# Attention with agents and a two-layer product on one core: the main loop in the order it is written, with jobs at fixed places

## The chip, the cores and the metric

The kernel runs on one core of a Trainium2 chip. A core has a matrix engine (TensorE, PE in the profile; its weight loads are PEld), VectorE (DVE), ScalarE (ACT), GpSimd (POOL) and a queue that issues transfers (SyncE, SP). Each engine takes its own instructions strictly in order; between engines they wait on semaphores. TensorE writes to PSUM, which VectorE and ScalarE read. The metric is the time of one execution on the device in microseconds, lower is better.

## The reference

Four batches of 12480 tokens with 128 channels, 49 agents, and a hidden width of 2048:

```python
def sm(a, b):                       # softmax over the last axis
    s = scale * (a @ b.transpose(0, 2, 1))
    e = np.exp(s - s.max(-1, keepdims=True))
    return e / (e.sum(-1, keepdims=True) + 1e-09)
agent_v = sm(agents, k) @ v         # phase 1: each batch, over all keys
x = (sm(q, agents) @ agent_v).reshape(49920, 128)
h = x @ w_in                        # phase 2: all tokens
out = (h - np.tanh(h)) @ w_out
```

## The kernel before

`sm(q, agents) @ agent_v @ w_in` is computed as `sm(q, agents) @ (agent_v @ w_in)`, so that the first product of phase 2 has only 49 rows to sum over; `aw` is that small matrix of one batch. Products that need more than the fast f32 format gives are made from a rounded part and a rest: `awh` and `awl`, `wo_h` and `wo_l`, `gh` and `gl`, stacked or added as several matmuls.

The tokens are cut into 100 blocks of 500 (25 a batch), and a block's hidden width into 8 pairs of 128 columns. One **step** is one block and one column pair, 800 steps in all; two blocks make a pair of blocks, 16 steps, and `pos` counts 0 to 15 in it. A step has on TensorE the first product (`m1`, L536/L537, 4 matmuls into the PSUM tile `h`, three buffers), on ScalarE tanh and its square (`act`, L546 `y` and L548 `z`), on VectorE the multiplication `g = h * z` (L551), on GpSimd the rounding `gh` of `g` (`high`, L580), on VectorE the rest `gl = g - gh` (`low`, L586), and on TensorE the second product (`m2`, L599 to L601, 6 matmuls into `misc`). The tanh difference is approximated by `h` times a scaled square. All steps of the first block and one step in every even block are **f32 steps**: no rounding and no rest, 2 f32 matmuls (recorded as 4, L597) with `g` itself. That step is column pair 7 (`PLAIN_PAIR`).

Beside the steps run **jobs**, Python generators that are advanced by one `yield` a step:

- the queries of the next pair of blocks (`q_softmax`): 64 small matmuls (L492), maximum (L500), copy (L501), subtraction on GpSimd (L503), exponential (L505), sum, reciprocal and multiplication on VectorE (L507 to L510, the normalization), rounding (L513) and rest on GpSimd (L515); then a transpose per block (L523, L528);
- phase 1 of the next batch, three jobs started in each pair of blocks: 13 score jobs (64 small matmuls L278, a copy and a maximum), the maximum over all, 13 value jobs (subtraction on GpSimd L321, exponential L329, 16 matmuls L341, an addition on VectorE L354), then `aw` of that batch in four projections (L456 to L460).

PSUM tiles of jobs and the accumulator of the second product share two buffers (`misc`).

The order on each engine comes from a scheduler that simulates the program, within limits that the kernel gives it: `hold` puts an instruction behind another on the same engine, `burst` and `streamed` tie small matmul groups of jobs to the stream of large ones on TensorE, `issue_order` fixes the early part. The products of the steps themselves are free to pass one another.

Of the kernel before, what the change touches and what calls it, by code (L numbers as in the profile page):

```python
# [57 lines left out]
PLAIN_PAIR = NCH // 2 - 1  # L58
PLAIN_EVERY = 2
LAG1 = 1  # L60
LAG2 = 2
# [3 lines left out]
SPLIT = (8, 9, 11, 13)  # L65
QL = 0
QS = 5
T0 = 13
T1 = 3
KS = (6, 9, 14)  # L70
VS = (2, 5, 9)
# [26 lines left out]
class Build:  # L98
    def __init__(self, ctx, tc, aps):
# [8 lines left out]
        self.stream = None  # L108
# [86 lines left out]
    def phase1(self, b):  # L195
# [36 lines left out]
        def scores(g):  # L232
# [41 lines left out]
            first = self.count()  # L274
# [4 lines left out]
            self.burst(first)  # L279
# [9 lines left out]
        def max_in():  # L289
# [4 lines left out]
            nc.vector.tensor_reduce(m, part, axis=AX.X, op=ALU.max)  # L294
            ps = self.misc()
# [17 lines left out]
        def av(g):  # L313
# [8 lines left out]
            if b:  # L322
                self.hold(first, self.gh_at, (ET.Pool,))
# [4 lines left out]
            first = self.count()  # L328
            nc.scalar.activation(e3, e3, AF.Exp, scale=SCALE)  # L329
            if b:  # L330
                self.hold(first, self.act_at, (ET.Activation,))
                yield
            yield
            if b:
                ps = self.misc()
                first = self.count()
# [11 lines left out]
                self.burst(first)  # L348
# [90 lines left out]
    def project(self, b, bound):  # L439
        nc = self.nc  # L440

        def part(c, lo, hi):
# [16 lines left out]
            nc.scalar.copy(h, ps)  # L459
            nc.vector.tensor_tensor(awl[:A2, sl], ps, h.bitcast(F32), ALU.subtract)  # L460
# [20 lines left out]
    def q_softmax(self, halves, qt, res, TT=TT):  # L481
        nc = self.nc
        yield
        ps = self.misc()
        first = self.count()
# [7 lines left out]
        self.burst(first)  # L493
        yield
# [7 lines left out]
        yield  # L502
        nc.gpsimd.tensor_tensor(ev, ev, m[:TT, :, None].broadcast_to([TT, GT, A]), ALU.subtract)  # L503
        yield
        nc.scalar.activation(ev, ev, AF.Exp, scale=SCALE)  # L505
        yield
# [4 lines left out]
        yield  # L511
        pp = self.small.tile([128, GT, A2], F32R, tag="pp", name="pp")
        nc.scalar.copy(pp[:TT, :, :A], ev)  # L513
        yield
        nc.gpsimd.tensor_tensor(pp[:TT, :, A:], ev, pp[:TT, :, :A].bitcast(F32), ALU.subtract)  # L515
        res.append(pp)
# [26 lines left out]
    def act(self, h, w):  # L543
# [5 lines left out]
        self.act_at = self.last_name()  # L549
        g = self.wtile("g", NB["g"])[:, : 2 * w]  # L550
        nc.vector.tensor_tensor(self.pair(g), h, self.pair(z), ALU.mult)  # L551
# [26 lines left out]
    def high(self, g):  # L578
        gh = self.wtile("gh", NB["gh"])[:, : g.shape[1]].bitcast(F32R)
        self.nc.gpsimd.tensor_scalar(gh, g, 1.0, 0.0, ALU.mult, ALU.add)  # L580
        self.gh_at = self.last_name()
        return gh
# [38 lines left out]
    def queued(self, first):  # L621
        return [i for i in list(self.nc.cur_bb.bb.instructions)[first:] if i.engine == ET.PE]

    def after(self, i, names):
        info = mybir.DependencyInfo(mybir.DependencyClass.NoSync, mybir.DependencyReason.DATA)
        for name in names:
            self.tc.add_manual_dep(i, name, info, reason="order on TensorE")
# [309 lines left out]
```

## Time and profile before

| | us |
|---|---|
| median of 3 runs | 2156.54 (2156.36 to 2161.76) |
| profiled execution, its own time | 2154.2 |
| its span in the profile | 2152.4 |
| busy in the span: TensorE, weight loads | 2089.7 (97%), 1635.8 (76%) |
| VectorE, ScalarE, GpSimd | 1989.5 (92%), 1795.2 (83%), 1378.3 (64%) |

Until 57.7 us phase 1 of the first batch runs. The first multiplication `g` starts there. Then the 50 pairs of blocks follow, the last one at 2106.9 us. From 1723.4 us on there is no more phase 1 to do, only steps and query jobs. Reading the profile: a row of the groups gives line, engine, operation, tiles and shapes, then count, busy us, mean ns of one, and idle time of the engine before them with what ended it. A row of the waits is who waited, for whom, us in total, times, and longest. A matmul's record covers its way through the array, so that consecutive records overlap.

### The profile page before, as it was taken

Reading aid. Unit: us, or ns where it says so; the run is one execution under the profiler, and the core shown is the slowest. Engines: PE = TensorE matmul, PEld = TensorE weight load, DVE = VectorE, ACT = ScalarE, POOL = GpSimd, SP = SyncE. Lnnn points to the kernel's source line nnn. Section 1 sums busy time; section 2 is a strip of 40 time slices with the busy share of each in tenths; the row PEclk is TensorE's granted clock in tenths of the full one; section 3 lists DMA queues with packets and bytes.
Section 4 is the critical chain, followed back from the end, with each engine's and each line's share of the span. In section 5 each row is a group of like instructions: output and inputs, shape, how many; then the busy total and the mean of one; then the engine's idle time right before and its main releaser. Section 6 shows DMA issues by size and latency. Waiting matters only on the chain.

```text
span 2152.4 us, 38228 instructions
## 1 busy us (share of the span) xinstructions
PE 2089.7 (97%) x14885; PEld 1635.8 (76%) x14885; DVE 1989.5 (92%) x2028; ACT 1795.2 (83%) x2097; POOL 1378.3 (64%) x896
## 2 busy tenths in 40 slices
PE   8999999999999999999999999999999999999998
PEld 7577777777777777777777777877777788888886
DVE  7999998889998999889999999998989999999998
ACT  3888887788788888888888888888878989989897
POOL 0365576666665566666666656767766777777776
PEclk9999999999999999999999999999999999999999
DMA  9221102111111111112001110121000000010000
GB/s 355 91 67 62 52 29 60 59 50 40 36 53 59 52 58 40 59 44 65 31 20 59 59 52 20 49 69 41 20 29 30 20 31 28 20 39 20 30 11 21
DMA packets 65358, 109.21 MB, mean 51 GB/s; under 512 B 3984, under 2 KB 44176, under 8 KB 65168
## 3 DMA queue, kind: packets, MB, share of 16 engines
q1 hardware_dynamic: 65168, 106.68, 15.1%
q8 instruction: 119, 1.95, 0.4%
q14 instruction: 71, 0.58, 0.1%
HBM read 81.10 MB, written 25.56 MB: 50 GB/s over the span
## 4 chain that ended last, share of the span: by engine, by line
PE 70%; DVE 15%; POOL 6%; issue 6%; ACT 3%; DMA 0%; POOLq 0%; DVEq 0%; SPq 0%; ACTq 0%
PE h L536 13%; PE h L537 12%; PE misc L599 12%; PE misc L601 12%; PE misc L600 11%; DVE g L551 8%; POOL gh L580 5%; DVE gl L586 4%; PE misc L597 3%; PE misc L341 2%; ACT z L548 1%; PE misc L492 1%; ACT y L546 1%; PE misc L523 1%; PE h L249 1%
## 5 line engine op out<-in xcount | busy, mean ns | idle before, releaser
L580 POOL TENSOR_SCALAR gh<-g 128x1000 fp32r<-128x1000 f32 (+1 forms) x743 | 1218.6, 1640 | 611.2 <-DVE g L551 499.9
L586 DVE TENSOR_TENSOR gl<-g,gh 128x1000 fp32r<-128x1000 f32 (+1 forms) x743 | 937.2, 1262 | 100.4 <-POOL gh L580 91.4
L551 DVE TENSOR_TENSOR g<-h,z 128x1000 f32<-128x1000 f32 (+1 forms) x800 | 945.4, 1190 | 27.9 <-ACT z L548 24.0
L546 ACT ACTIVATE y<-h 128x1000 f32<-128x1000 f32 (+1 forms) x800 | 798.7, 1000 | 118.6 <-PE h L537 113.8
L548 ACT ACTIVATE z<-y 128x1000 f32<-128x1000 f32 (+1 forms) x800 | 831.3, 1041 | 53.4 <-DVE g L551 35.4
L536 PE MATMUL h<-pT,awh 98*128 98x500 f32 (+1 forms) x1600 | 654.5, 409 | 7.9 <-DVE g L551 7.8
L537 PE MATMUL h<-pT,awl 98*128 98x500 f32 (+1 forms) x1600 | 621.2, 388 | 0.0
L599 PE MATMUL misc<-gh,wo_l 128*128 128x500 f32 (+1 forms) x1486 | 594.6, 400 | 5.9 <-ACT o L783 3.0
L601 PE MATMUL misc<-gl,wo_h 128*128 128x500 f32 (+1 forms) x1486 | 584.9, 394 | 7.7 <-DVE gl L586 7.6
L600 PE MATMUL misc<-gh,wo_h 128*128 128x500 f32 (+1 forms) x1486 | 579.1, 390 | 0.0
L536 PEld LDWEIGHTS h<-pT,awh 98*128 98x128 f32 x1600 | 300.7, 188 | 96.3 <-DVE g L551 24.8
L537 PEld LDWEIGHTS h<-pT,awl 98*128 98x128 f32 x1600 | 302.6, 189 | 69.9 <-issue 12.4
L599 PEld LDWEIGHTS misc<-gh,wo_l 128*128 128x128 f32 x1486 | 280.5, 189 | 83.6 <-POOL gh L580 21.3
L601 PEld LDWEIGHTS misc<-gl,wo_h 128*128 128x128 f32 x1486 | 279.7, 188 | 78.4 <-DVE gl L586 23.4
L600 PEld LDWEIGHTS misc<-gh,wo_h 128*128 128x128 f32 x1486 | 280.2, 189 | 49.3 <-issue 1.1
L503 POOL TENSOR_TENSOR qe<-qe,qm 126x392 f32<-126x392 f32 x50 | 65.5, 1309 | 61.4 <-ACT qe L501 61.4
L515 POOL TENSOR_TENSOR pp<-qe,pp 126x392 fp32r<-126x392 f32 x50 | 51.6, 1031 | 67.3 <-ACT pp L513 67.3
L597 PE MATMUL misc<-g,wo_f 128*128 128x500 f32 (+1 forms) x196 | 91.4, 588 | 0.0
L783 ACT ACTIVATE o<-misc 128x500 f32<-128x500 f32 (+1 forms) x100 | 57.9, 579 | 36.4 <-PE misc L597 21.6
L501 ACT COPY qe<-misc 126x392 f32<-126x392 f32 x50 | 24.1, 482 | 74.2 <-DVE qm L500 74.2
L528 ACT CAST pT<-misc 98x500 fp32r<-98x500 f32 (+1 forms) x100 | 57.1, 572 | 11.3 <-PE misc L523 9.7
L492 PEld LDWEIGHTS misc<-ag,qt 128*32 128x32 f32 (+1 forms) x3200 | 39.3, 112 | 24.9 <-issue 17.6
(103 smaller groups left out, 829.0 us busy)
## 6 DMA issues: line engine op xcount, KB each, us to landing
kt<-kT SPq DMA_DIRECT2D x48, 512.0 KB, 3.9
qt<-qT SPq DMA_DIRECT2D x46, 500.0 KB, 3.5
outT<-o SPq DMA_DIRECT2D x46, 500.0 KB, 2.6
v<-v SPq DMA_DIRECT2D x36, 512.0 KB, 4.0
vt<-v SPq DMA_DIRECT2D x12, 512.0 KB, 7.5
raw<-w_in SPq DMA_DIRECT2D x4, 512.0 KB, 9.2
v<-w_out SPq DMA_DIRECT2D x4, 512.0 KB, 7.8
qt<-qT SPq DMA_DIRECT2D x4, 490.0 KB, 3.7
```

What stands on the lines that cost most here:

```text
L503: nc.gpsimd.tensor_tensor(ev, ev, m[:TT, :, None].broadcast_to([TT, GT, A]), ALU.subtract)
L536: nc.tensor.matmul(h[:, c, :w], aw[0][:A2, sl], pT[:A2, :w], start=True, stop=False)
L537: nc.tensor.matmul(h[:, c, :w], aw[1][:A2, sl], pT[:A2, :w], start=False, stop=True)
L546: nc.scalar.activation(self.pair(y), h, AF.Tanh, scale=TSC)
L548: nc.scalar.activation(z, y, AF.Square)
L551: nc.vector.tensor_tensor(self.pair(g), h, self.pair(z), ALU.mult)
L580: self.nc.gpsimd.tensor_scalar(gh, g, 1.0, 0.0, ALU.mult, ALU.add)
L586: self.nc.vector.tensor_tensor(gl, g, gh.bitcast(F32), ALU.subtract)
L597: nc.tensor.matmul(acc[:, :w], wf[:, c * C : (c + 1) * C], gh[:, x], start=first, stop=last)
L599: nc.tensor.matmul(acc[:, :w], self.wo_l[:, f, :], gh[:, x], start=first, stop=False)
L600: nc.tensor.matmul(acc[:, :w], self.wo_h[:, f, :], gh[:, x], start=False, stop=False)
L601: nc.tensor.matmul(acc[:, :w], self.wo_h[:, f, :], gl[:, x], start=False, stop=last)
```

## The change

The order of the loop is written out, and the engines keep it: at the end `issue_order` now fixes VectorE, GpSimd and TensorE for the whole program (before: early parts only), and `burst`, `streamed` and their bookkeeping are gone. The loop body is rewritten to fit. Step k has, in this order: jobs are advanced; tanh and square of step k+1 (`squares`); multiplication of step k (`product`); its rounding; rest of step k-1 (`low(1)`); second product of step k-1 (`out`); first product of step k+3 (`first_product`, `AHEAD = 3`); new jobs are started. Before, it was: first product of step k, jobs, tanh, square, multiplication and rounding of step k, rest of step k-1, second product of step k-3.

So jobs stand on VectorE between a subtraction (of two steps back) and a multiplication. Further:

- the f32 step is column pair 6 instead of 7, and the queries' normalization stands at `pos` 6 to 7 (`QS`, `QGAPS`);
- 87 of the 743 roundings are done by ScalarE (`by_act`): at the step after which a value job starts, and at `pos` 8 (`QLOW`), where the rest of the queries stands on GpSimd;
- GpSimd's two-tile subtractions of value jobs (L321) and of the queries' rest wait on a semaphore for the multiplication (`wait_for`), where a value job's subtraction was before only held behind the last rounding in GpSimd's own order;
- jobs start at other positions: `KS`, `VS`, `T0`, `T1`; the queries' load, still issued at `pos` 0, is used three steps later instead of six; an output block is copied two steps after its last product.

```diff
-PLAIN_PAIR = NCH // 2 - 1
+PLAIN_PAIR = 6
-QS = 5
-T0 = 13
-T1 = 3
-KS = (6, 9, 14)
-VS = (2, 5, 9)
+QS = 2
+QGAPS = (1, 1, 0, 2, 1, 1, 1)
+QLOW = 8
+T0 = 11
+T1 = 13
+KS = (3, 5, 13)
+VS = (1, 3, 11)
...
             (nc.gpsimd if b else nc.vector).tensor_tensor(e3, sv, top, ALU.subtract)
             if b:
-                self.hold(first, self.gh_at, (ET.Pool,))
+                self.wait_for(first, self.mul_at)
...
+        first = self.count()
         nc.gpsimd.tensor_tensor(pp[:TT, :, A:], ev, pp[:TT, :, :A].bitcast(F32), ALU.subtract)
+        if gaps != (1,) * 7:
+            self.wait_for(first, self.mul_at)
...
-    def high(self, g):
+    def high(self, g, act=False):
         gh = self.wtile("gh", NB["gh"])[:, : g.shape[1]].bitcast(F32R)
-        self.nc.gpsimd.tensor_scalar(gh, g, 1.0, 0.0, ALU.mult, ALU.add)
-        self.gh_at = self.last_name()
+        if act:
+            self.nc.scalar.copy(gh, g)
+        else:
+            self.nc.gpsimd.tensor_scalar(gh, g, 1.0, 0.0, ALU.mult, ALU.add)
...
+    def wait_for(self, first, name):
+        info = mybir.DependencyInfo(mybir.DependencyClass.Sync, mybir.DependencyReason.DATA)
+        for i in list(self.nc.cur_bb.bb.instructions)[first:]:
+            self.tc.add_manual_dep(i, name, info, reason="order at the shared port")
...
-            h = foreground(n, i)
+            if p + 1 < npair and pos in (T0, T1):
+                live.append(t_job(2 * p + 2 + (pos == T1)))
             nxt = []
...
-            rest(n, i, h)
-            low(LAG1)
+            self.hold(first, self.act_at, (ET.Activation,))
+            squares(k + 1)
+            values = nv - NG - 2 < len(kq) < nv
+            begin = kq and n and pos in (VS if values else KS)
+            by_act = values and begin and kq[0] is not None or p and pos == QLOW and p + 1 < npair
+            product(k, by_act)
+            low(1)
...
-            out(LAG2)
+            out(k)
             if n == 0 and i == HP - 1:
-                self.issue_order(ET.DVE, at)
                 self.issue_order(ET.Activation, at)
-                self.issue_order(ET.PE, early)
-            if p + 1 < npair:
+            first_product(k + AHEAD)
+            if p and p + 1 < npair:
...
+        self.issue_order(ET.DVE, at)
+        self.issue_order(ET.Pool, early)
+        self.issue_order(ET.PE, early)
         self.loads_first(early)
```

Three places show what moved. The first is VectorE in the second block of a pair with value jobs (steps 130 to 134; `gl` and `qm` as above, `acc` is the value job's addition). Before:

```order
L586 TENSOR_TENSOR gl_4393<-g_4364,gh_4366 128x1000
L551 TENSOR_TENSOR g_4418<-h_4407,z_4416 128x1000
L586 TENSOR_TENSOR gl_4422<-g_4389,gh_4391 128x1000
L586 TENSOR_TENSOR gl_4444<-g_4418,gh_4420 128x1000
L551 TENSOR_TENSOR g_4440<-h_4430,z_4438 128x1000
L500 TENSOR_REDUCE qm_4522<-misc_4459 126x8
L551 TENSOR_TENSOR g_4496<-h_4454,z_4494 128x1000
```

and in the change:

```order
L589 TENSOR_TENSOR gl_4460<-g_4402,gh_4404 128x1000
L494 TENSOR_REDUCE qm_4476<-misc_4419 126x8
L551 TENSOR_TENSOR g_4486<-h_4389,z_4454 128x1000
L589 TENSOR_TENSOR gl_4490<-g_4456,gh_4458 128x1000
L551 TENSOR_TENSOR g_4516<-h_4414,z_4484 128x1000
L589 TENSOR_TENSOR gl_4520<-g_4486,gh_4488 128x1000
L348 TENSOR_TENSOR acc_994<-acc_994,misc_4503 113x129
L551 TENSOR_TENSOR g_4540<-h_4468,z_4514 128x1000
```

Two subtractions stood side by side; now one multiplication stands between any two, and the jobs stand behind a subtraction.

The second is GpSimd at the same steps (L321 is a value job's subtraction, `qe` the queries'). Before:

```order
L580 TENSOR_SCALAR gh_4366<-g_4364 128x1000
L321 TENSOR_TENSOR s_861<-s_861,mb_3284 128x392
L580 TENSOR_SCALAR gh_4391<-g_4389 128x1000
L580 TENSOR_SCALAR gh_4420<-g_4418 128x1000
L580 TENSOR_SCALAR gh_4442<-g_4440 128x1000
```

and in the change:

```order
L321 TENSOR_TENSOR s_993<-s_993,mb_3291 128x392
L584 TENSOR_SCALAR gh_4404<-g_4402 128x1000
L321 TENSOR_TENSOR s_993<-s_993,mb_3291 128x392
L497 TENSOR_TENSOR qe_4477<-qe_4477,qm_4476 126x392
L584 TENSOR_SCALAR gh_4488<-g_4486 128x1000
```

Each L321 stands in the place of a rounding, which ScalarE does (those of `g_4376` and `g_4456`).

The third is TensorE, some ten steps earlier: the second product of one step and the first product of another. Before:

```order
L537 MATMUL h_4105<-pT_3976,awl_646 128x500
L599 MATMUL misc_3959<-gh_4006,wo_l_88 128x500
L600 MATMUL misc_3959<-gh_4006,wo_h_87 128x500
L536 MATMUL h_4127<-pT_3976,awh_645 128x500
L537 MATMUL h_4127<-pT_3976,awl_646 128x500
L536 MATMUL h_4127<-pT_3976,awh_645 128x500
L537 MATMUL h_4127<-pT_3976,awl_646 128x500
L601 MATMUL misc_3959<-gl_4064,wo_h_87 128x500
```

and in the change:

```order
L534 MATMUL h_4092<-pT_3859,awl_646 128x500
L602 MATMUL misc_3946<-gh_4082,wo_l_88 128x500
L603 MATMUL misc_3946<-gh_4082,wo_h_87 128x500
L604 MATMUL misc_3946<-gl_4106,wo_h_87 128x500
L602 MATMUL misc_3946<-gh_4082,wo_l_88 128x500
L603 MATMUL misc_3946<-gh_4082,wo_h_87 128x500
L604 MATMUL misc_3946<-gl_4106,wo_h_87 128x500
L533 MATMUL h_4114<-pT_3859,awh_645 128x500
```

The matmul with `gl` stood behind the next first product; now the second product is one piece, and the first product waits behind it.

127 lines of the change are left out of this document (49 added, 78 removed).

## The prediction

> **What bounds the kernel now.** I read the windows view first, cut at the starts of `g<-h,z` products, so that each stretch holds whole pairs of query blocks (16 steps). Columns: length, then busy us and instruction count of TensorE, weight loads, VectorE, ScalarE and GpSimd, granted clock, DMA share, GB/s.
>
> ```profile
> 57.70:146.30 88.60, 84.53 (x689) 58.02 (x688) 84.67 (x94) 75.30 (x92) 44.80 (x33) 1.00 0.22 65
> 146.30:1723.40 1577.10, 1536.45 (x11178) 1195.02 (x11177) 1448.09 (x1454) 1318.00 (x1529) 1019.35 (x669) 1.00 0.15 46
> 1723.40:2106.90 383.50, 383.50 (x2302) 309.25 (x2301) 377.14 (x362) 347.97 (x391) 284.06 (x171) 1.00 0.07 25
> ```
>
> There are two regimes. In the last ten pairs TensorE has no idle time: 383.5 us, 38.35 us per pair. The 37 pairs before them, which also carry the key and value jobs of the next batch, take 42.6 us each with 40.7 us of open TensorE idle. Matmuls overlap in the records, so busy time hides part of a stall; I count from start to start. Timeline of TensorE around a value job and a score job, and the ends of an undisturbed row of 13 matmuls (start, length):
>
> ```profile
> 392.40 0.38 PE L537 MATMUL h<-pT,awl 98*128 98x500 f32 x1
> 392.71 1.09 PE L341 MATMUL misc<-v,s 128*64 128x129 f32 x16
> 393.73 0.49 PE L599 MATMUL misc<-gh,wo_l 128*128 128x500 f32 x1
> 394.06 0.39 PE L600 MATMUL misc<-gh,wo_h 128*128 128x500 f32 x1
> ...
> 163.31 0.39 PE L601 MATMUL misc<-gl,wo_h 128*128 128x500 f32 x1
> 163.63 0.90 PE L278 MATMUL misc<-ag,kt 128*32 128x49 f32 x64
> 164.46 0.49 PE L599 MATMUL misc<-gh,wo_l 128*128 128x500 f32 x1
> 164.79 0.40 PE L600 MATMUL misc<-gh,wo_h 128*128 128x500 f32 x1
> ...
> 1007.15 0.39 PE L536 MATMUL h<-pT,awh 98*128 98x500 f32 x1
> 1009.86 0.39 PE L600 MATMUL misc<-gh,wo_h 128*128 128x500 f32 x1
> ```
>
> A 500-column matmul starts (1009.86 - 1007.15)/12 = 0.226 us after the one before it. A value job costs 394.06 - 392.40 - 0.45 = 1.21 us of TensorE, a score job 164.79 - 163.31 - 0.45 = 1.03; the queries' 64 small matmuls (L492) have the score job's form, 1.03. What stood in the middle stretch, by form (count | busy, mean ns | idle before):
>
> ```profile
> L536 PE MATMUL h<-pT,awh 98*128 98x500 f32 x1136 | 463.6, 408 | 6.2 <-DVE g L551 6.2
> L599 PE MATMUL misc<-gh,wo_l 128*128 128x500 f32 x1067 | 429.7, 403 | 5.3 <-ACT o L783 3.0 <-POOL gh L580 1.7
> L523 PE MATMUL misc<-identr,pp 126*98 126x126 f32 x296 | 30.9, 227 | 0.0
> L278 PE MATMUL misc<-ag,kt 128*32 128x49 f32 x2032 | 29.1, 209 | 0.0
> L341 PE MATMUL misc<-v,s 128*64 128x129 f32 x294 | 40.7, 280 | 15.9 <-ACT qe L501 15.9
> L456 PE MATMUL misc<-w_in,avs 128*98 128x512 f32 x24 | 12.2, 591 | 0.0
> ```
>
> Sum at full pace: L536/L537 twice 1136 and L599 to L601 three times 1067, 5473 x 0.226 = 1237; the narrower last block of each batch about 50; 37 f32 steps, one a pair, at 1.8 (a late pair's rest: 38.35 less 154 x 0.226, 1.03 and 0.7 for the transposes of L523, four by four at twice 0.35) = 67; queries 37 x 1.03 = 38; transposes 37 x 0.7 = 26; scores 2032/64 x 1.03 = 33; values 36.75 x 1.21 = 44; projections 24 x 0.43 = 10. Together 1505. So about **72 us of the middle stretch are TensorE stalls**, 2.0 per pair; by the same prices the last stretch has about none. The waits view of the middle stretch says who ended them:
>
> ```profile
> DVE gl L586 <- POOL gh L580: 82.9, 107, 1.9
> PEld misc L341 <- ACT qe L501: 21.8, 14, 2.4
> PEld h L536 <- DVE g L551: 20.3, 39, 2.2
> PEld misc L599 <- POOL gh L580: 19.5, 45, 1.0
> PEld misc L601 <- DVE gl L586: 16.3, 34, 0.9
> ```
>
> Two causes, 56 us for late g, gh and gl, 22 us for value jobs that wait for ScalarE's copy of the queries' scores, which holds a PSUM buffer (weight-load idle, which overlaps a little with issue time). Behind late gl stands VectorE waiting for GpSimd's rounding, 82.9 us. Why the rounding is late, on both engines at one place:
>
> ```profile
> 1002.41 1.19 DVE L551 TENSOR_TENSOR g<-h,z 128x1000 f32<-128x1000 f32 x1
> 1003.55 1.20 DVE L586 TENSOR_TENSOR gl<-g,gh 128x1000 fp32r<-128x1000 f32 x1
> 1004.66 1.19 DVE L551 TENSOR_TENSOR g<-h,z 128x1000 f32<-128x1000 f32 x1
> 1005.77 1.19 DVE L586 TENSOR_TENSOR gl<-g,gh 128x1000 fp32r<-128x1000 f32 x1
> 1007.89 1.20 DVE L586 TENSOR_TENSOR gl<-g,gh 128x1000 fp32r<-128x1000 f32 x1 [0.92 <-POOL gh L580]
> ...
> 1002.48 1.03 POOL L580 TENSOR_SCALAR gh<-g 128x1000 fp32r<-128x1000 f32 x1 [2.52 <-PE misc L601]
> 1003.79 1.85 POOL L580 TENSOR_SCALAR gh<-g 128x1000 fp32r<-128x1000 f32 x1 [0.28 <-PE misc L601]
> 1006.04 1.81 POOL L580 TENSOR_SCALAR gh<-g 128x1000 fp32r<-128x1000 f32 x1 [0.40 <-PE h L537]
> ```
>
> The rounding takes 1.03 us beside a multiplication and 1.8 beside a subtraction, where it ends 0.89 us after the subtraction (1005.64 after 1004.75, 7.85 after 6.96): it stands still meanwhile. At 1006.96 a second subtraction follows the first, waits 0.92 us and VectorE is lost for that long.
>
> **The change, part by part.** *VectorE* (the first pair of order listings above). Subtractions no longer stand side by side. Each subtraction now has a multiplication between itself and the last, and a job stands in front of a multiplication. The cycle by the rows above: subtraction at 0, multiplication at 1.11, next subtraction at 2.22; the rounding ends at 1.20 + 0.89 = 2.09 and is seen 0.04 later (7.85 to 7.89). It fits with 0.09 us to spare, and TensorE's 10 x 0.226 = 2.26 per step leaves 0.04 more. VectorE per pair: 31 x 1.11 = 34.4, queries 2, jobs at most 3 x 0.56 = 1.7: 38.1 against 42.0 of TensorE work in a job pair, 36.4 against 38.35 in a late one. VectorE doesn't bind.
>
> *Query normalization beside the f32 step.* The f32 step moves from pair 7 to 6, where the normalization stands; that step has no rounding, so nothing collides. The multiplication in the last stretch, and over the whole run (count: ns least/median/most):
>
> ```profile
> L510 DVE TENSOR_TENSOR qe<-qe,qs 126x392 f32<-126x392 f32 x10 | 13.8, 1383 | 0.0
> ...
> L510 DVE TENSOR_TENSOR qe<-qe,qs x50: 547/566/1387, 42.6 to 2091.6; 126x392 f32<-126x392 f32 x50
> ```
>
> 1.38 us against 0.57: 0.8 us per late pair. VectorE there has 2 us in reserve, so I price it at nothing; without that cover it would be 10 x 0.8 = 8 us.
>
> *GpSimd and ScalarE* (second pair of listings). Each L321 stands where a rounding stood; that rounding (of g_4376 and g_4456) went to ScalarE. 87 of 743 move. The new waits of L321 and of the queries' rest for a multiplication cost nothing: behind them on GpSimd stands the next step's rounding, which needs the multiplication after that. No row shows a ScalarE copy of 128x1000 into fp32r; the nearest is the square:
>
> ```profile
> L546 ACT ACTIVATE y<-h 128x1000 f32<-128x1000 f32 (+1 forms) x800 | 798.7, 1000 | 118.6 <-PE h L537 113.8
> L548 ACT ACTIVATE z<-y 128x1000 f32<-128x1000 f32 (+1 forms) x800 | 831.3, 1041 | 53.4 <-DVE g L551 35.4
> L528 ACT CAST pT<-misc 98x500 fp32r<-98x500 f32 (+1 forms) x100 | 57.1, 572 | 11.3 <-PE misc L523 9.7
> L329 ACT ACTIVATE s<-s 128x392 f32<-128x392 f32 x48 | 24.6, 523 | 5.8 <-DVE s L321 4.0 <-POOL s L321 1.8
> ```
>
> I take 1.04, with 1.00 (tanh) and 1.15 (L528 twice, its fixed part too) as ends. ScalarE per pair by durations: 16 x 2.04 = 32.7, two output and two transpose copies at 0.57 = 2.3, the queries' three at 0.52 = 1.5, one rounding 1.04: 37.5 against 38.35. A value pair adds three exponentials (0.52) and three roundings: 42.2 against 42.0. By starts a step is less, since a tanh starts before the square ahead of it ends (1041 + 1000 ns is an upper bound), but **ScalarE is now the tight engine of a value pair**.
>
> *TensorE* (third pair of listings). The second products of step k-1 now stand whole in front of the first products of step k+3; before, the parts with gl were pushed behind the next first products. What waits behind a late gl is thus everything. Between the end of h[k]'s matmuls and the use of gl[k-1] TensorE has two steps and two matmuls, 2 x 2.26 + 0.45 = 5.0 us. The chain in that time is tanh 1.00, square 1.04, multiplication 1.19, subtraction 1.20 and four handoffs of 0.05: 4.6. Reserve 0.4 us. A ScalarE job in between (0.5 to 1.04) uses it up unless ScalarE was ahead, and it gains 2.26 - 2.04 = 0.2 per step. At positions 8 to 10 of each pair a 0.52 cast, a 1.04 rounding and a 0.57 output copy come in three steps, behind the f32 step, which costs TensorE 0.3 us more and spares VectorE a subtraction: 2.1 us of jobs less 0.4 of reserve, less 3 x 0.2, less 0.3 and 0.4 that the f32 step gives: 0.4 us of stall per pair. In value pairs three more roundings (1.56 with their exponentials, against 1.21 that TensorE gets) add 3 x 0.35, rounded down to 0.6: 1.0 us.
>
> *The sum.* Middle stretch: 72 us of stalls go; 12 value pairs x 1.0 + 25 x 0.4 = 22 come, so -50. Last stretch: 10 x 0.4 = +4. The first 57.7 us, the 88.6 after them (VectorE 84.67 busy there, the decoding of the weights is unchanged; bounds -4 and +5) and the tail: 0. No DMA moves past another except the queries' load, three steps before its use instead of six: 7 us, and such a load lands after 3.5:
>
> ```profile
> qt<-qT SPq DMA_DIRECT2D x46, 500.0 KB, 3.5
> ```
>
> 2154.2 - 46 = 2108 us for the profiled execution (its own time, 1.8 us above its span; the median of the runs is 2.3 above it). I forecast **2108 us**.
>
> **Rivals.**
> *(A) All stalls go*, handoffs overlap better than I count: 2154 - 72 = 2082. For it: the last stretch runs without stalls at the same VectorE alternation. Against: ScalarE's 42.2.
> *(B) Weight loads are the real limit, TensorE has room even in the late pairs.* Their loads fill 309.25 of 383.50 us, 81%. VectorE's 36.4 would then set late pairs and 38.1 the others: -2 x 10 - 4.5 x 37 = -187, 1967. Against it: 0.226 us from start to start wherever nothing waits, and TensorE without idle for 383.5 us. The Trainium skill, Perfetto Trace Analysis, Identifying the Most-Contended Engine, says that matmul busy time is a poor measure of headroom and weight-load share a good one; by that rule a fifth is left, and the constant start-to-start time here disagrees.
> *(C) ScalarE binds the value pairs and lags elsewhere*: a copy takes 1.15 and ScalarE never gains a step back, so value pairs lose 2.0 us instead of 1.0 and the other 35 lose 0.9 instead of 0.4: 12 + 17 on the forecast, 2137. For it: 42.2 against 42.0. Against: tanh and square overlap at their ends.
> *(D) Nothing moves*: gl comes 0.13 us too late in every step with a rest of the 37 pairs, with a whole second product and the next first product behind it: 15 x 37 x 0.13 = 72 us again, 2150 to 2160. For it: a reserve of 0.4 us that one job uses up. Against: the late pairs ran with the same chain.
> *(E) Slower: the roundings get in first.* If gh[k-1] ends after multiplication k, GpSimd goes on with gh[k] at once and the subtraction, ready in the same moment, stands still for 1.03 us. One such place before:
>
> ```profile
> 418.62 1.69 DVE L586 TENSOR_TENSOR gl<-g,gh 128x1000 fp32r<-128x1000 f32 x1
> ```
>
> The margin is 0.09 us, and it fails wherever GpSimd has a job or ScalarE's rounding is late, up to 7 steps of a job pair, 3 of a late one. VectorE: 38.1 + 7 = 45.1 in job pairs, 36.4 + 3 = 39.4 in late ones: +2.5 x 37 + 1 x 10 = 2257; with 5 and 2, 2172. It decides from about 4.5 per job pair. Against: one hit is repaid, since the next rounding is then early. The Trainium skill, SBUF — State Buffer, SBUF: two separate sides, says that the shared port pair goes to whichever starts first, for the whole instruction; the 1.85 and the 1.69 above agree.
>
> **How the numbers follow.** Forecast (2088 to 2128) 0.55, A 0.10, B 0.02, C 0.13, D 0.07, E 0.13. A measurement here tells 0.3% (6.5 us) from no change. Faster: forecast, A, B, C = 0.80; same 0.07; slower 0.13. Range: from 12 us below A (2070) to D's 2150; B and E with the far half of D stay out. The likeliest case alone is 2088 to 2128.
>
> **What would show it.** Right: the subtraction's waits for GpSimd fall from 82.9 to under 20 us in the middle; roundings all near 1.8 or 1.03; value jobs no longer wait for the queries' copy; late pairs at 38 to 39 us; ScalarE busy up by about 90 us (87 x 1.04). Wrong: subtractions of 1.7 us and more in most pairs (E); TensorE idle that ends at gl in every step, or ScalarE above 95% in value pairs (C, D); late pairs below 37.5 (B).

## The result, and the profile after

The changed kernel takes 2227.68 us (median; 2226.41 to 2227.98), the kernel before on the same chip 2157.02 us: a ratio of **1.032** (1.0304 to 1.0339). It is 71 us slower where the prediction said 2108 us and faster. The profiled execution has a span of 2224.6 us against 2152.4.

The windows view of the changed kernel, cut at the same multiplications as in the prediction: the first two pairs of blocks, the 37 pairs with jobs of the next batch, the last ten pairs (columns as there).

```profile
58.90:158.60 99.70, 88.97 (x639) 60.17 (x638) 84.92 (x94) 79.07 (x95) 47.37 (x33) 0.98 0.16 47
158.60:1777.30 1618.70, 1550.29 (x11232) 1188.63 (x11231) 1443.30 (x1454) 1402.26 (x1603) 989.98 (x592) 1.00 0.14 45
1777.30:2179.30 402.00, 389.90 (x2302) 306.04 (x2301) 379.21 (x361) 360.44 (x400) 271.90 (x161) 1.00 0.07 24
```

Every stretch loses: 1.2 us ahead of the first multiplication, 11.1 in the first two pairs (99.7 against 88.6), 41.6 in the middle (1618.7 against 1577.1), 18.5 in the last ten (402.0 against 383.5), and nothing behind them. Within the middle, counted from multiplication to multiplication, pairs with three score jobs take 45.2 to 48.4 us (41.5 to 43.9 before); the nine pairs with three value jobs take 43.1 to 43.2 (42.3 to 46.0 before), and six of them gain. By the prediction's price of the middle's TensorE work, 1505 us, its stalls are 114 us now and were 72. The granted clock does not explain it: it is 1.00 in the middle and in the last stretch, as before. VectorE's busy time in the middle has hardly moved (1443 against 1448), so VectorE did not get more work. ScalarE's rose by 84 us, most of it the 75 roundings that it does there. What rose on VectorE is waiting. The waits view of the changed kernel, whole span (who waited for whom: us in total, times, longest):

```profile
ACT y L543 <- PE h L534: 214.4, 432, 1.7
PEld misc L604 <- DVE gl L589: 175.1, 231, 2.0
...
PE misc L604 <- DVE gl L589: 89.1, 106, 1.6
DVE s L280 <- ACT s L279: 68.4, 38, 2.6
...
DVE qm L494 <- PE misc L487: 31.4, 34, 2.3
...
DVE gl L589 <- POOL gh L584: 29.0, 50, 0.9
```

TensorE waits for `gl` (175.1 us on the weight-load side, 89.1 on the matmul side of the same waits), and behind it ScalarE waits for TensorE (214.4, it was 113.8). The old cause has shrunk: the subtraction's wait for GpSimd is 29.0 us in the whole span, where it was 82.9 in the middle alone. Two new ones stand in its place, both of VectorE in front of a **maximum** that a job brings: 68.4 us for score jobs, 31.4 for the queries. The groups view of the kernel before shows the same two maxima; the last column is VectorE's idle time ahead of them:

```profile
L500 DVE TENSOR_REDUCE qm<-misc 126x8 f32<-126x392 f32 x50 | 27.9, 558 | 1.7 <-PE misc L492 1.7
...
L282 DVE TENSOR_REDUCE s<-misc 128x49 f32<-128x392 f32 (+1 forms) x39 | 20.8, 535 | 0.0
```

1.7 and 0.0 us. The scheduler had put these maxima where their input lay ready.

### One place, on four engines

The timelines of TensorE, VectorE, GpSimd and ScalarE of the changed kernel in a late pair (start, length, and in brackets idle time and what ended it):

```profile
1985.51 0.39 PE L604 MATMUL misc<-gl,wo_h 128*128 128x500 f32 x1
...
1987.10 0.39 PE L534 MATMUL h<-pT,awl 98*128 98x500 f32 x1
1987.42 0.90 PE L487 MATMUL misc<-ag,qt 128*32 128x49 f32 x64
...
1994.97 0.50 PE L604 MATMUL misc<-gl,wo_h 128*128 128x500 f32 x1 [1.21 <-DVE gl L589]
...
1986.40 1.19 DVE L589 TENSOR_TENSOR gl<-g,gh 128x1000 fp32r<-128x1000 f32 x1
1988.39 0.57 DVE L494 TENSOR_REDUCE qm<-misc 126x8 f32<-126x392 f32 x1 [0.80 <-PE misc L487]
1988.87 1.19 DVE L551 TENSOR_TENSOR g<-h,z 128x1000 f32<-128x1000 f32 x1
1989.97 1.19 DVE L589 TENSOR_TENSOR gl<-g,gh 128x1000 fp32r<-128x1000 f32 x1
1991.08 1.19 DVE L551 TENSOR_TENSOR g<-h,z 128x1000 f32<-128x1000 f32 x1
1992.90 2.01 DVE L589 TENSOR_TENSOR gl<-g,gh 128x1000 fp32r<-128x1000 f32 x1 [0.62 <-POOL gh L584]
...
1990.06 1.81 POOL L497 TENSOR_TENSOR qe<-qe,qm 126x392 f32<-126x392 f32 x1 [1.58 <-ACT qe L495]
1991.84 2.03 POOL L584 TENSOR_SCALAR gh<-g 128x1000 fp32r<-128x1000 f32 x2
...
1989.51 0.47 ACT L495 COPY qe<-misc 126x392 f32<-126x392 f32 x1
```

Read from the top. On TensorE the job's small matmuls (L487) stand behind a second product, whose first use of `gl` starts at 1985.51, and a first product. They end at 1988.3. VectorE started the next `gl` at 1986.40 and is free for the maximum at 1987.59. It waits 0.80 us, and the multiplication behind it, whose inputs are ready, waits with it. That is the first loss. The second follows from the first: the queries' copy (1989.51) and with it GpSimd's subtraction (1990.06) now start just behind a VectorE subtraction (1989.97) instead of beside a multiplication. GpSimd's takes 1.81 us, the rounding behind it is late, two roundings run back to back (1991.84, 2.03 for both), and the second, which starts near 1992.85, gets in just ahead of the VectorE subtraction of 1992.90, which takes 2.01 us in place of 1.19. TensorE gets its `gl` 1.21 us late, with the rest of that second product and the next first product behind it, and so also the tanh and the multiplication that need this first product.

The second timeline, of VectorE and ScalarE, shows a score job's maximum:

```profile
684.37 1.19 DVE L589 TENSOR_TENSOR gl<-g,gh 128x1000 fp32r<-128x1000 f32 x1
688.16 0.57 DVE L280 TENSOR_REDUCE s<-misc 128x49 f32<-128x392 f32 x1 [2.59 <-ACT s L279]
688.64 1.19 DVE L551 TENSOR_TENSOR g<-h,z 128x1000 f32<-128x1000 f32 x1
...
684.44 1.04 ACT L545 ACTIVATE z<-y 128x1000 f32<-128x1000 f32 x1
685.67 1.01 ACT L543 ACTIVATE y<-h 128x1000 f32<-128x1000 f32 x1 [0.19 <-PE h L534]
686.71 1.04 ACT L545 ACTIVATE z<-y 128x1000 f32<-128x1000 f32 x1
687.66 0.47 ACT L279 COPY s<-misc 128x392 f32<-128x392 f32 x1
```

The square for the multiplication of 688.64 was done at 685.48. But the maximum stands ahead of it, and the maximum waits for ScalarE's copy of the same scores (both read one PSUM tile, and the copy is written first). The copy in turn stands on ScalarE behind a whole tanh and square of the *next* step. ScalarE is the one engine of the four whose order the change leaves to the scheduler behind the first block: the loop writes the copy ahead of that tanh, and the scheduler put it behind. VectorE sits idle for 2.59 us with work ready behind the wait.

**Theory J (job waits):** jobs stand in the fixed order where their input isn't ready; each such wait on VectorE makes `gl` late, and TensorE, which runs only some 0.4 us behind `gl` (0.36 at the place above, from the end of the subtraction of 1983.96 to the matmul of 1985.51), stalls with everything behind it. **Rivals:** R, the 87 roundings make ScalarE lag; F, the moved f32 step; S, the loop's pace is set elsewhere and these waits only fill idle time.

### The profile page after: what moved, and what is told of

It is laid out like the page before. It is cut to its first block, busy times and chain, and to the rows that moved or that the text cites. A ratio compares the mean times of both kernels' runs of the same rounds, so it can differ in the third digit from the quotient of the medians.

```text
span 2224.6 us, 37436 instructions
## 1 busy us (share of the span) xinstructions
PE 2113.7 (95%) x14885; PEld 1627.5 (73%) x14885; DVE 1987.3 (89%) x2028; ACT 1896.3 (85%) x2184; POOL 1340.2 (60%) x809
## 4 chain that ended last, share of the span: by engine, by line
PE 69%; DVE 13%; ACT 12%; issue 4%; POOL 2%; DMA 0%; POOLq 0%; SPq 0%; DVEq 0%; ACTq 0%
PE misc L604 13%; PE h L534 13%; PE h L533 13%; PE misc L602 12%; PE misc L603 11%; DVE gl L589 6%; ACT y L543 5%; DVE g L551 4%; ACT z L545 4%; PE misc L600 3%; PE misc L336 2%; POOL gh L584 1%; PE h L249 1%; PE misc L520 1%; DVE s L280 1%
## 5 line engine op out<-in xcount | busy, mean ns | idle before, releaser
L584 POOL TENSOR_SCALAR gh<-g 128x1000 fp32r<-128x1000 f32 (+1 forms) x656 | 1091.9, 1667 | 669.2 <-DVE g L551 633.9
L543 ACT ACTIVATE y<-h 128x1000 f32<-128x1000 f32 (+1 forms) x800 | 803.1, 1004 | 221.1 <-PE h L534 214.4
L589 DVE TENSOR_TENSOR gl<-g,gh 128x1000 fp32r<-128x1000 f32 (+1 forms) x743 | 927.0, 1248 | 35.4 <-POOL gh L584 29.0
L604 PE MATMUL misc<-gl,wo_h 128*128 128x500 f32 (+1 forms) x1486 | 602.1, 405 | 89.3 <-DVE gl L589 89.1
L533 PE MATMUL h<-pT,awh 98*128 98x500 f32 (+1 forms) x1600 | 644.8, 403 | 3.2 <-ACT awh L453 1.5
L604 PEld LDWEIGHTS misc<-gl,wo_h 128*128 128x128 f32 x1486 | 279.4, 188 | 229.4 <-DVE gl L589 175.1
L497 POOL TENSOR_TENSOR qe<-qe,qm 126x392 f32<-126x392 f32 x50 | 82.2, 1644 | 122.5 <-ACT qe L495 122.5
L510 POOL TENSOR_TENSOR pp<-qe,pp 126x392 fp32r<-126x392 f32 x50 | 91.5, 1830 | 54.5 <-DVE g L551 45.4
L582 ACT CAST gh<-g 128x1000 fp32r<-128x1000 f32 x87 | 88.8, 1020 | 5.7 <-DVE g L551 5.6
L321 POOL TENSOR_TENSOR s<-s,mb 128x392 f32<-128x392 f32 (+1 forms) x39 | 70.3, 1803 | 29.3 <-DVE g L551 29.3
L280 DVE TENSOR_REDUCE s<-misc 128x49 f32<-128x392 f32 (+1 forms) x39 | 21.2, 544 | 68.4 <-ACT s L279 68.4
```

Of the source, the lines that this page charges most:

```text
L533: nc.tensor.matmul(h[:, c, :w], aw[0][:A2, sl], pT[:A2, :w], start=True, stop=False)
L543: nc.scalar.activation(self.pair(y), h, AF.Tanh, scale=TSC)
L589: self.nc.vector.tensor_tensor(gl, g, gh.bitcast(F32), ALU.subtract)
L604: nc.tensor.matmul(acc[:, :w], self.wo_h[:, f, :], gl[:, x], start=False, stop=last)
```

## The experiments

All times are medians; each ratio is against the kernel before, run beside it. The kernel before had medians of 2154.3 to 2157.2 us beside the different runs, so a difference between two rows of a few microseconds says nothing.

| kernel | us | ratio (interval) |
|---|---|---|
| the change | 2227.7 | 1.0322 (1.0304 to 1.0339) |
| qm_later | 2168.5 | 1.0059 (1.0042 to 1.0076) |
| score_later | 2169.6 | 1.0065 (1.0048 to 1.0082) |
| second_lag | 2111.3 | 0.9793 (0.9776 to 0.9809) |
| free_order | 2162.9 | 1.0034 (1.0022 to 1.0047) |
| max_later | 2109.3 | 0.9786 (0.9770 to 0.9802) |
| max_later_lag | **2096.9** | **0.9731** (0.9714 to 0.9747) |
| no_act | 2243.9 | 1.0414 (1.0397 to 1.0432) |
| plain7 | 2259.2 | 1.0484 (1.0467 to 1.0502) |
| sub_later | 2214.4 | 1.0274 (1.0254 to 1.0293) |
| free_max_lag | 2168.3 | 1.0062 (1.0037 to 1.0086) |
| max_first | 2170.6 | 1.0069 (1.0052 to 1.0086) |

### qm_later: the queries' maximum one step later

```diff
-QGAPS = (1, 1, 0, 2, 1, 1, 1)
+QGAPS = (1, 2, 0, 1, 1, 1, 1)
```

> The maximum, copy and subtraction of the queries' scores stand one step later on VectorE, ScalarE and GpSimd; nothing else moves. Theory (job waits): in the changed kernel VectorE waits 31.4 us in 34 of the 50 pairs in front of this maximum, because its small matmuls stand on TensorE behind the first products of the same step; in-order TensorE then passes the delay on to the next multiplication. So the wait falls below 5 us, a late pair goes from 40.2 to 38.5-39.3 us, and the time falls by 40 to 85 us: 2143 to 2188. Rival R (the 87 roundings on ScalarE cost the time) and rival F (the moved f32 step costs it): no change, 2221 to 2234. Rival S (the pace is set elsewhere in the loop and this wait only fills idle time): the wait goes and the time stays within 10 us.

Measured: 2168.5 us, 59 less than the change. The windows view, middle and last ten pairs:

```profile
157.30:1736.90 1579.60, 1527.55 (x11232) 1193.81 (x11231) 1423.60 (x1453) 1398.17 (x1603) 1015.53 (x592) 1.00 0.15 46
1736.90:2121.50 384.60, 384.60 (x2302) 308.13 (x2301) 373.13 (x362) 360.13 (x400) 279.87 (x161) 1.00 0.07 25
```

The timelines of VectorE and GpSimd at the place that answers to the one above:

```profile
1940.65 0.56 DVE L494 TENSOR_REDUCE qm<-misc 126x8 f32<-126x392 f32 x1
1941.12 1.19 DVE L551 TENSOR_TENSOR g<-h,z 128x1000 f32<-128x1000 f32 x1
1942.23 1.48 DVE L589 TENSOR_TENSOR gl<-g,gh 128x1000 fp32r<-128x1000 f32 x1
...
1941.81 0.84 POOL L497 TENSOR_TENSOR qe<-qe,qm 126x392 f32<-126x392 f32 x1 [0.19 <-ACT qe L495]
```

No wait in front of the maximum; GpSimd's subtraction runs beside the multiplication in 0.84 us; the late pairs are back at 38.5 us. The 59 us are more than the 31.4 of the wait, since the collision behind it nearly goes too: the slow subtraction is down to 1.48 us, from 2.01. R, F and S expected no gain here, so none of them can be the cause of this part. The score jobs' wait stays, and even grows:

```profile
DVE s L280 <- ACT s L279: 82.4, 39, 2.6
```

### score_later and max_first: the score jobs' maximum

score_later has one `yield` between the copy and the maximum; max_first swaps the two lines.

```diff
             nc.scalar.copy(st["s"][:, g * GT * A : (g * GT + n) * A], ps[:, : n * A])
+            yield
             nc.vector.tensor_reduce(
```

> The maximum of a score job stands one step behind ScalarE's copy of the same scores, not in the step of the copy. Theory (job waits): VectorE's 68.4 us in front of this maximum (38 places, 1.8 us each, waiting for the copy) fall below 8 us; a score pair goes from 46.9 to 43-44 us; 12 to 13 pairs carry three of them, so the time falls by 35 to 60 us: 2168 to 2193. Rivals R and F: no change, 2221 to 2234. Rival S: the wait goes and the time stays within 10 us.

Measured: 2169.6 us, 58 less than the change. The waits view, and the windows view of the last ten pairs:

```profile
DVE s L281 <- ACT s L279: 3.9, 12, 0.3
```

```profile
1721.00:2123.00 402.00, 389.90 (x2302) 306.18 (x2301) 379.30 (x362) 360.19 (x400) 271.51 (x161) 1.00 0.07 24
```

The wait is gone. Pairs of the middle with three score jobs take 42.7 to 42.9 us now. The last ten pairs, which have no score jobs, stay at 402.0 us, and pairs with three value jobs stay at 43.1.

> The changed kernel with the maximum of a score job written ahead of ScalarE's copy of the same scores, in the same step: VectorE then waits for the job's matmuls alone, and the copy waits for the maximum. It splits the 1.8 us that VectorE waits in front of this maximum into the part that TensorE's order makes (0.8 to 0.9 us, as for the queries' maximum) and the part that the copy adds by standing behind tanh and square. Theory: the 68.4 us fall to 30-40 us, now ended by the job's matmuls, and the time falls by about half of the 58 us that moving the maximum a whole step gave: 2190 to 2210. If the copy is all of it: 2165 to 2180. If the copy adds nothing: within 7 us of 2228.

Measured: 2170.6 us, the same as a whole step later. Its waits view has, in place of the 68.4 us:

```profile
DVE s L279 <- PE misc L277: 16.9, 25, 1.0
```

The expectation of half was wrong. The copy is nearly all of it, 51.5 of 68.4 us; with the maximum written first, VectorE takes the scores as soon as the matmuls are done, and the copy, which nobody needs soon, waits on ScalarE for a maximum, which costs nothing that shows against score_later. Two lines in the other order are worth 57 us.

### second_lag: a longer reserve on TensorE

```diff
-        def out(k):
-            while r2:
+        def out(k, keep=1):
+            while len(r2) > keep:
...
-        out(len(steps))
+        out(len(steps), 0)
```

> The second product of step k-1 stands one step later on TensorE, behind the first product of step k+4 in place of k+3; VectorE, ScalarE and GpSimd keep their order. Theory (job waits, with a reserve of only 0.4 us between the end of the first product and the use of gl): the reserve grows by one TensorE step, 2.27 us, so a wait of 0.9 or 1.8 us on VectorE no longer reaches TensorE: its stalls fall from 173 us to under 80, the time to 2110-2150, though the waits on VectorE themselves stay. If instead ScalarE or VectorE are bound by their own work (rival C or E of the prediction), the time stays within 15 us of 2228, and TensorE's idle time ends at the multiplication's weight load in place of gl's.

Measured: 2111.3 us. It does not touch the jobs and still takes back 116 us: a late `gl` now finds TensorE with another step of work in hand. Lines of the waits view and the windows of the middle and the last ten pairs:

```profile
DVE s L280 <- ACT s L279: 32.6, 24, 2.6
...
PEld h L533 <- DVE g L551: 31.5, 40, 2.1
...
DVE qm L494 <- PE misc L487: 13.9, 17, 1.0
...
PEld misc L604 <- DVE gl L589: 1.6, 3, 0.9
```

```profile
149.50:1670.00 1520.50, 1510.41 (x11232) 1198.92 (x11231) 1428.39 (x1453) 1382.25 (x1603) 974.82 (x592) 1.00 0.15 48
1670.00:2063.80 393.80, 385.05 (x2302) 309.07 (x2301) 375.56 (x362) 360.29 (x401) 268.81 (x161) 1.00 0.07 24
```

TensorE's waits for `gl` fall from 175.1 us to 1.6. In the last ten pairs this is the reserve alone: VectorE still waits for the queries' maximum in each of them (9.7 us in all, 7.9 in the change) and each still has its subtraction of 2.0 us, yet a pair goes from 40.2 us to 39.4. What is left there are first products that wait for a multiplication (13.0 us). In the middle, against the expectation, the waits in front of the maxima shrink too, from 63.3 to 32.6 us and from 22.5 to 4.2. Nothing but TensorE's order was edited, so this comes of the lag, but how was not followed up, and the 98 us gained there are not split into the two parts. This speaks against rival C of the prediction as the cause of the loss: ScalarE has the same 87 roundings here.

### free_order: the scheduler's order again

```diff
             if n == 0 and i == HP - 1:
+                self.issue_order(ET.DVE, at)
                 self.issue_order(ET.Activation, at)
+                self.issue_order(ET.PE, early)
...
-        self.issue_order(ET.DVE, at)
-        self.issue_order(ET.Pool, early)
-        self.issue_order(ET.PE, early)
```

> The orders along the whole program on VectorE, GpSimd and TensorE are taken out (ScalarE's and those of the first block stay as in the kernel before); the 87 roundings on ScalarE, the moved f32 step, the later jobs of the queries and the waits of GpSimd's subtractions stay. Theory (the fixed order puts jobs where they must wait): the time comes back to within 25 us of the kernel before, 2135 to 2182, with paired subtractions again. Rivals R and F (roundings on ScalarE, f32 step): the loss stays, 2210 to 2235.

Measured: 2162.9 us. Everything else of the change is still in it, so R and F cannot account for the 71 us. Paired subtractions are back with it (121 of them; 102 before, one in the change), and so is the old wait of `gl`:

```profile
DVE gl L589 <- POOL gh L584: 113.0, 132, 1.3
```

### max_later and max_later_lag: both maxima, and both repairs

max_later joins qm_later and score_later; max_later_lag adds second_lag.

> Both maxima one step later: those of the queries and those of the score jobs. Theory (job waits): the two places are in different steps and pairs, so the gains add: 2227.7 - 59.2 - 58.1 = 2110, between 2100 and 2125, with late pairs at 38.4 us and score pairs at 41 to 42 us. If the two waits cover for each other (a common rest of the loop sets the pace as soon as one is gone), it stays between 2130 and 2165.

Measured: 2109.3 us, 118 less than the change where the two alone gave 59 + 58: they add, as two waits at different places do when each is paid in full. Pairs with three score jobs take 41.2 to 41.4 us and late pairs 38.5, as expected. Windows of the middle and the last ten pairs:

```profile
149.70:1679.00 1529.30, 1518.29 (x11305) 1197.79 (x11305) 1430.29 (x1455) 1394.18 (x1606) 1017.17 (x593) 1.00 0.15 48
1679.00:2063.60 384.60, 384.60 (x2302) 308.14 (x2301) 373.22 (x361) 360.34 (x400) 279.81 (x161) 1.00 0.07 25
```

> Both maxima one step later, and the second product one step later on TensorE as well. Theory (job waits through a short reserve): both attack the same stalls from two ends, so the gains (117 us and 116 us) do not add: TensorE without any stall would need 2228 - 167 = 2061 by its floor, and with the remaining stalls at the first product (about 27 us in the middle) 2080 to 2105; late pairs 38.3 to 38.6 us in place of 39.4. If the lag costs something of its own (first products that wait for a multiplication to give back their PSUM buffer), late pairs stay at 39 us or more and the time at 2100 to 2115.

Measured: **2096.9 us, 2.7% faster than the kernel before and the fastest of all**:

```profile
146.50:1665.90 1519.40, 1511.03 (x11239) 1203.24 (x11238) 1420.81 (x1455) 1381.14 (x1605) 1006.64 (x593) 1.00 0.15 48
1665.90:2048.10 382.20, 382.20 (x2302) 309.73 (x2301) 370.80 (x361) 354.73 (x400) 267.62 (x161) 1.00 0.07 25
```

The gains of the two repairs (118 and 116) do not add, since both are spent on the same stalls. The middle is 14 us above its price of 1505, the late pairs are at 38.2 us, a little below what was expected.

### no_act and plain7: the rivals R and F

```diff
-            product(k, by_act)
+            product(k, False)
```

```diff
-PLAIN_PAIR = 6
+PLAIN_PAIR = 7
```

> The changed kernel with all 743 roundings on GpSimd; orders and jobs as in the change. Theory (job waits): the 87 roundings on ScalarE are no cause of the loss; taking them off gives nothing back where VectorE waits for a maximum, and in value jobs GpSimd then carries a 0.9 us subtraction and a rounding in the same step: 2222 to 2250. Rival R (the roundings on ScalarE cost the time, by making it lag): the time falls by 40 us or more, to 2188 or less.

> The changed kernel with the f32 step back at pair 7 of the even blocks. Theory (job waits): the place of this step is no cause; the queries' multiplication then runs beside a rounding (up to 0.8 us more in each of 48 pairs): 2222 to 2265. Rival F (the moved step costs the time): falls by 40 us or more, to 2188 or less.

Measured: 2243.9 and 2259.2 us, both slower than the change. The roundings on ScalarE are worth 16 us and the moved f32 step 32 us, in the change as it stands: neither is the cause of the loss, both are gains inside it. For the f32 step, a late pair of plain7 on VectorE suggests why:

```profile
1980.77 0.55 DVE L501 TENSOR_REDUCE qs<-qe 126x8 f32<-126x392 f32 x1
...
1982.03 0.57 DVE L504 TENSOR_TENSOR qe<-qe,qs 126x392 f32<-126x392 f32 x1
1982.52 1.20 DVE L551 TENSOR_TENSOR g<-h,z 128x1000 f32<-128x1000 f32 x1
...
1984.73 2.30 DVE L551 TENSOR_TENSOR g<-h,z 128x1000 f32<-128x1000 f32 x2
```

The four instructions of the normalization hold the multiplication for 1.75 us (1982.52 less 1980.77). In the change two multiplications follow at once, without the f32 step's subtraction between them, and 1.1 us is made up before the next `gl`. In plain7 one more subtraction comes first, behind all of the 1.75 us, and the two multiplications follow only then (1984.73). That this order makes the 32 us is a reading of one place; no run splits it. The multiplication of the normalization itself takes 0.57 us in both.

### sub_later: the wait and the collision apart

```diff
-QGAPS = (1, 1, 0, 2, 1, 1, 1)
+QGAPS = [1, 1, 1, 1, 1, 1, 1]
```

> The changed kernel with only GpSimd's subtraction of the queries' maximum one step later; maximum and copy stay. It splits the 59 us that moving all three gave back. In the changed kernel this subtraction starts 0.1 us behind a VectorE subtraction and takes 1.81 us in place of 0.84, the next two roundings follow each other, and the second gets in ahead of a VectorE subtraction that takes 2.01 us. If VectorE's wait for the maximum (0.9 us) is the whole cause: within 10 us of 2228. If the collision is the whole cause: 2160 to 2175 and late pairs at 38.4 us. Theory now (both, about half each): 2185 to 2210, late pairs at 39.2 to 39.6 us, subtractions over 1.3 us gone in late pairs, the wait for the maximum still there.

Measured: 2214.4 us, 13 less than the change and 4 outside what was expected. Windows of the middle and the last ten pairs:

```profile
158.90:1771.20 1612.30, 1540.08 (x11232) 1192.40 (x11231) 1433.74 (x1453) 1401.92 (x1603) 1022.00 (x592) 1.00 0.14 45
1771.20:2163.30 392.10, 389.88 (x2302) 306.09 (x2301) 375.64 (x361) 360.49 (x401) 279.14 (x161) 1.00 0.07 24
```

GpSimd's subtraction takes 0.84 us again. In a late pair the time splits about as expected: of the 1.7 us that qm_later gave back (40.2 to 38.5), 1.0 comes with the collision at the old place (40.2 to 39.2) and 0.7 with the rest, the wait above all. But the slow subtraction, expected gone, stays in each late pair, at 1.73 us in place of 2.01: in the timelines GpSimd's subtraction now starts 0.17 us ahead of a VectorE subtraction (1981.01 and 1981.18) and holds that one up. So the 1.0 is what this edit takes away, not the whole collision. In the middle it is worth 6 us of the 39 that qm_later gained there (1618.7 to 1579.6); the score jobs' wait for the copy grows meanwhile, from 68.4 to 83.8 us, so this 6 is no clean price either.

### free_max_lag: is the order worth anything by itself?

The edit of free_order, made to max_later_lag.

> Both maxima and the second product one step later, as in the fastest kernel so far (2096.9 us), but without the orders along the whole program on VectorE, GpSimd and TensorE. If the fixed order is worth something once the jobs stand where their inputs are ready (subtraction and multiplication always in turn): 2110 to 2140, with 80 or more subtractions of over 1.3 us and late pairs of 39 to 40 us. If the order as such is worth nothing and the placement of the maxima and of the second product is all: within 7 us of 2097.

Measured: 2168.3 us, above even what was expected for a useful order. Late pairs are at 39.8 us and 122 subtractions take over 1.3 us, both as expected for that case. With the scheduler's order the moved maxima and the lag bring nothing (free_order has 2162.9 without them); with the fixed order they bring 131 us. So the three fixed orders together are worth 71 us (2168.3 less 2096.9), but only when the jobs stand where their inputs are. How much of this is the turn of subtraction and multiplication on VectorE, and how much the orders of GpSimd and TensorE, was not split, and which of the scheduler's placements eats the gain was not followed up.

## Why the prediction was wrong

**The step that failed** is the price of a job on VectorE: "VectorE per pair: ... jobs at most 3 x 0.56 = 1.7 ... VectorE doesn't bind". The maximum does take 0.57 us. But in a fixed order an instruction costs its wait as well as its length, and the wait was never asked for: 0.57 + 0.9 for the queries (31.4 us over 34), 0.57 + 1.8 for a score job (68.4 over 38). So VectorE, which had the shorter sum, still set the pace: its waits made `gl` late, TensorE stalled for it, and the middle has 114 us of stalls where the forecast had 22. The rows for the queries' wait were there. The order listings ahead of the prediction show `qm` directly behind a subtraction, and the prediction's own prices give TensorE's path from the first use of a `gl` to the end of the job's matmuls: four matmuls of the second product and four of the first at 0.226 and a job of 1.03 make 2.8 us. VectorE, from the end of the same `gl`, reaches the maximum after one multiplication and one subtraction, 2.22 us. The difference, and the 0.4 us by which TensorE starts behind `gl`, come to 1.0 us, about the measured 0.9. For a score job the prediction also missed that the maximum waits for ScalarE's copy, which max_first shows to be most of it.

**The reserve of 0.4 us** was about the right size (0.36 at the place shown) and put to the wrong use. It was charged against ScalarE's jobs only, and any wait on VectorE comes out of it too. second_lag, which enlarges it by a step and edits nothing else, took back 116 of the 120 us by which the forecast was missed, in the middle in part because the waits themselves shrank.

**The rest of the sum held in total.** With the two maxima moved and nothing else, the middle is 1529.3 us (forecast 1577.1 - 50 = 1527), the last stretch 384.6 (383.5 + 4 = 387.5), the whole 2109.3 (2108). That it meets to 1 us is partly luck, for not every term holds. Pairs with three value jobs take 43.0 us, as priced (42.0 and 1.0 of stall; that ScalarE makes the 1.0 is not shown). Pairs with three score jobs take 41.2 to 41.4, the bare price of their TensorE work (38.35 + 3 x 1.03 = 41.4), and late ones 38.5: the 0.4 us of stall that the forecast gave each is hardly there. The middle is still 24 us above its price, and where the rest of that lies was not followed up.

Point by point, first from the waits and the groups of the changed kernel's middle stretch:

```profile
DVE gl L589 <- POOL gh L584: 20.5, 37, 0.6
```

```profile
L582 ACT CAST gh<-g 128x1000 fp32r<-128x1000 f32 x75 | 76.6, 1021 | 5.7 <-DVE g L551 5.6
```

- *Waits of the subtraction for GpSimd* under 20 us in the middle: 20.5 us, from 82.9. As good as right. The value jobs' 21.8 us for the queries' copy are gone from the waits. Right.
- *Roundings on GpSimd* near 1.8 or 1.03 us: right, the median is 1.84.
- *A rounding on ScalarE* at 1.04 us: 1.02. ScalarE's busy time rose by 101 us over the span (1795.2 to 1896.3), expected about 90. Rival C, that ScalarE binds, was wrong: ScalarE itself waits 214.4 us for TensorE, it is busy for 39.4 of the 43.1 us of a pair with three value jobs (91%, where its sign was above 95%), and taking the roundings off it costs 16 us (no_act).
- *The f32 step moved, at nothing, 8 us without its cover*: wrong in size. Its place is worth 32 us, and not through the 1.38 us of the normalization's multiplication, which is 0.57 in either place. That the step without a subtraction pays for the normalization's 1.75 us is the likely reason, not a tested one.
- *The first two pairs and the time ahead of them, at 0*: they lost 12.3 us; score jobs run there too. max_later has 90.0 us in the first two pairs, against 88.6 before. The granted clock of 0.98 is not the cause, for max_later has it there too.
- *Late pairs at 38 to 39 us*: 40.2. Wrong, by the queries' maximum and its collision.
- *Rival D* has the right last link, a late `gl` with a whole second product behind it, but not the cause: it charged 0.13 us to every step, where, from multiplication to multiplication, 13 of 16 steps of the late pair shown run at 2.6 us or less and three, those with the queries' maximum, the collision and the normalization, at 3.6 to 3.8.
- *Rival E* comes nearest by its numbers: the measured time lies between its 2172 and 2257, and its sign came true, a subtraction of 1.7 us or more in 47 of the 50 pairs. Its mechanism is there at one place per pair: a late rounding on GpSimd goes on at once and holds up a subtraction for 2.01 us. It was set off by a job's subtraction on GpSimd, which E allowed for and the forecast's sum left out. But E is only a part of the loss (sub_later takes back 1.0 us of a late pair's 1.7 and 13 us in all). Its count, two to seven a pair, was too high: 53 of 743 subtractions took 1.7 us or more, 47 before the change. And the loss can go while they stay: score_later has 53 of them too and is 58 us faster, second_lag has 50 and is 116 us faster. The Trainium skill (SBUF — State Buffer, SBUF: two separate sides) says that a VectorE instruction with two SBUF inputs and a GpSimd instruction that reads SBUF share a port pair, which goes to whichever starts first. The 1.81 us beside a subtraction, which reads `g` and `gh`, and the 0.84 beside a multiplication, which reads `h` from PSUM, agree with that.

## What to carry to other kernels

When an order is fixed by hand, price each instruction of a side job twice: its length, and the time until its inputs are there, counted on the engine that makes them from the last event that both engines share. If that is later than the slot, move the job a step; where the job only reads what another engine copies, write the urgent reader first. And leave an in-order consumer a reserve longer than the waits of its producer: with 0.4 us, waits of 0.9 us became stalls, and with one step more TensorE's waits for `gl` fell from 175.1 to 1.6 us.

## What had not been expected

The same GpSimd subtraction (126x392) takes 0.84 us or 1.81 us, depending on whether it starts beside a VectorE multiplication or 0.1 us behind the start of a VectorE subtraction; a place that is right by its length alone can cost twice that. And in this program two readers of one PSUM tile on two engines keep the order in which they are written, which the trace shows as VectorE waiting for ScalarE: with the copy first VectorE waited 68.4 us, with the maximum first 16.9.
